# Expert weights five quarters ahead, raw words two parts ahead, a later exponential, and split words written in place

## The chip, the cores and the metric

The kernel runs on one core of a Trainium2 chip. The metric is the device time of one execution in microseconds (us), the median of several runs. Less is better.

## The reference

Three layers run one after the other. Only the second is touched by the change, and the third supplies the weights that one part of the change splits.

```python
# 1. gated recurrence over 768 steps, 4 batches x 8 heads of 40: x (3072 tokens, 320)
# 2. one of 8 experts per token (moe)
xn, en = x / (norm(x) + 1e-6), emb / (norm(emb) + 1e-6)
logits = xn @ en.T / tau
expert_idx = argmax(logits, axis=1)
gate_w = softmax(logits)[token, expert_idx]
for e in range(8):
    mask = expert_idx == e
    out[mask] = gate_w[mask, None] * (relu(x[mask] @ w1[e]) @ w2[e])   # 320 -> 1024 -> 320
# 3. rational layer (moe2): double words for w_in in memory
h = x @ w_in                                                          # 320 -> 2048
P = a0 + a1 h + a2 h^2 + a3 h^3;  Q = 1 + |b0||h| + |b1| h^2
out = (P / (Q + 1e-6)) @ w_out                                        # 2048 -> 320
```

The matrices w_in and w_out of layer 3 reach the core as 64-bit words, so each element is a low and a high 32-bit word side by side. Every product is made of three fast matmuls: each operand is split into a high part (rounded to the matmul's format) and a low part (the rest), and high by high, high by low and low by high are added in PSUM.

## The kernel before, in words

**Stages.** From 0 to about 216 us: the recurrence, the routing and the sorting of tokens by expert. From about 216 to 222 us: a branch on a register, around code for experts with more tokens than their buffer holds. That code is not run here, and each engine takes the branch by itself, once its own instructions before it are done. From there to about 458 us: the experts. Then to the end: the rational layer, with matmuls of 384 columns.

**The experts.** There are 64 blocks, n = 0 to 63. Block n is one eighth (`fb`) of the 1024 hidden units of expert `e`. The loop at the end of the listing issues per block, in this order: `gemm1(n)` (8 matmuls, L228, into `ph`), after which ScalarE (ACT) rounds the relu to `hh` (L1469) and VectorE (DVE) forms the rest `hl` (L1470); `gemm2(n-2)` (matmuls L1484 to L1486 into `yb`, with `hh` and `hl`); DMA loads; the transposes of the next expert's tokens (`x_prep`, PE L1107, ACT L1083 for the high part, DVE L1088 for the low part `xl`); the splitting of expert weights; and then a number of turns, each of which issues one step of the gates and one step of the split of layer 3's weights. Instructions keep this written order on every engine, and every engine runs its own list in order.

**Expert weights.** They come in quarters, two blocks each, 32 in all (`qq`). `w_load` issues four DMAs from SyncE (SP): `r1` (L162, L166 twice) and `r2` (L168), each with two buffers. `w_hi` makes the high parts `h1` and `h2` on ACT (L183, L185) three quarters ahead. `w_lo` makes the low parts `l1` and `l2` on GpSimd (POOL; L192, L196), partly on DVE at first. A buffer of `r1` or `r2` is free for a later load when both have read it. The load of quarter qq+4 is issued in the first block of quarter qq.

**Layer 3's weights.** `dbl` walks through 32 parts, 16 of w_in and 16 of w_out. `dbl_load` brings the raw words of a part into `raw` (L1357 and L1358, or L1361; two buffers; the load of part i+1 is issued after step 0 of part i). `dbl_split` has 8 steps: ACT L1386, DVE L1388, L1390, L1393, L1395, L1397 and L1406, and at last ACT L1409, or two stores from SP (L1412, L1413). L1393 reads the high words of `raw`, that is every second word, and L1395 its low words; L1395 writes `vt`, a buffer without gaps. `dbl_steps` spreads the steps over the blocks: most of them fall into blocks 8 to 40.

**The gates.** `gates` is a chain of short DVE steps on 128 rows, with one exponential on ACT (L1066) between L1064 and L1068. There is one such chain per expert, started in the last block of the expert before.

**Around it.** `x_load` gathers an expert's tokens (POOL), `y_scatter` scatters its results (POOL), and `y_load` (SP L1112) loads the sorted rows for layer 3 in block 52.

Of the kernel before, what the change touches and what calls it, by code (L numbers as in the profile page):

```python
# [8 lines left out]
F32 = mybir.dt.float32  # L9
F32R = mybir.dt.float32r  # L10
# [11 lines left out]
def kernel(  # L22
# [130 lines left out]
    def w_load(qq):  # L153
# [6 lines left out]
        cs = slice(qd * 256, (qd + 1) * 256)  # L160
        r1 = wsl.tile([128, 3, 256], F32, name="r1", tag="r1", bufs=2)
        nc.sync.dma_start(  # L162
            out=r1[:, 0:2, :], in_=w1r[bass.ds(e * DM, 256), cs].rearrange("(k p) f -> p k f", p=128)
        )
        for d in range(2):
            nc.sync.dma_start(out=r1[64 * d:64 * d + 64, 2, :], in_=w1r[bass.ds(e * DM + 256, 64), cs])  # L166
        r2 = wsl.tile([128, 2, DM], F32, name="r2", tag="r2", bufs=2)
        nc.sync.dma_start(  # L168
# [874 lines left out]

    def gates(pool, g, hd, tag, own=None):

# [18 lines left out]
        nc.vector.tensor_tensor(out=lg, in0=lg, in1=nrm.unsqueeze(2).broadcast_to([128, n, NE]), op=ALU.mult)  # L1064
        yield
        nc.scalar.activation(out=lg, in_=lg, func=AF.Exp)  # L1066
# [272 lines left out]
    with ExitStack() as mctx:  # L1339
        mp = mctx.enter_context(tc.tile_pool(name="mp", bufs=2, side="right"))  # L1340
        NB = NE * NFB
# [9 lines left out]
        def dbl_load(i):  # L1351
            raw = mp.tile([128, 3 * 128, 2], I32, name="raw", bufs=2)
            if i < 16:
# [12 lines left out]
        def dbl_steps(n):  # L1366

            a, c = (W0 * min(max(v - NFB, 0), 4 * NFB) + W1 * max(min(v, DE) - 5 * NFB, 0) for v in (n, NB))
            return a * ND * NS // c

        def dbl_split(i):
# [6 lines left out]

            if (i + 1) * NS <= dbl_steps(S3N[0]):
                st_ = vown[:, 0:n].bitcast(I32)  # L1380
            else:
                st_ = mp.tile([128, 384], I32, name="st_", bufs=1)[:, 0:n]
            vt = mp.tile([128, 384], F32, name="vt", bufs=1)[:, 0:n]
            ts, stt = nc.vector.tensor_scalar, nc.vector.scalar_tensor_tensor

            nc.scalar.activation(out=cf, in_=hi32.bitcast(F32), func=AF.Abs, scale=2.0**-112)  # L1386
            yield
            ts(out=st_, in0=c, scalar1=3, scalar2=-4096, op0=ALU.logical_shift_left, op1=ALU.bitwise_and)  # L1388
            yield
            stt(out=c, in0=hi32, scalar=-(2**31), in1=st_, op0=ALU.bitwise_and, op1=ALU.bitwise_or)  # L1390
            yield
# [24 lines left out]
        def dbl():  # L1416
            for i in range(ND):
                for k, _ in enumerate(dbl_split(i)):
                    if k == 0 and i + 1 < ND:
                        dbl_load(i + 1)  # L1420
                    yield
# [38 lines left out]
        def gemm1(n):  # L1460
# [5 lines left out]
            mm3(ph, h1, l1, slice(half * 128, half * 128 + 128), sx["x", e])  # L1466
            hh = mp.tile([128, 512], F32R, name="hh", bufs=4)[:, 0:c]
            hl = mp.tile([128, 512], F32R, name="hl", bufs=4)[:, 0:c]
            nc.scalar.activation(out=hh, in_=ph, func=AF.Relu)  # L1469
# [47 lines left out]
        x_load(1)  # L1517
        w_load(4)
        w_load(5)

# [32 lines left out]

        coef_load()
        dbl_load(0)
        dbls = dbl()

# [107 lines left out]
        for n in range(NB + LAG2):  # L1665
# [22 lines left out]
            if n >= NB:  # L1688
                continue
            if half == 0 and 5 < qq + 4 < 4 * NE:  # L1690
                w_load(qq + 4)
            if fb == 0 and 1 < e + 1 < NE:
# [20 lines left out]
            if n == 1 or fb == NFB - 1 and e + 1 < NE:  # L1713
                g = 0 if n == 1 else e + 1
                gs = slice(g * JS, g * JS + slots(g).stop)
                gsteps = gates(mp, gate[:, gs], head[:, gs, :], "g", vown[:, 384:] if g < NE - 1 else None)
            nd, ng = dbl_steps(n + 1) - dbl_steps(n), (4 if n > 5 else 6) if n else 0
            for i in range(max(nd, ng)):
# [132 lines left out]
```

## Time and profile before

| quantity | value |
|---|---|
| device time, median of 3 runs | 823.98 us (822.82 to 827.11) |
| the profiled execution's own device time | 823.25 us |
| its span in the profile | 821.2 us |
| mean granted clock of TensorE | 0.967 |
| busy: PE, DVE, POOL, ACT | 760.3, 713.6, 584.3, 488.8 us |

The span runs from the first to the last instruction that the profile shows; the device time is 2.05 us more. Times in the rows are microseconds from the start of the span. PE is the engine of the matmuls, and a stretch in which it is idle or at half its clock is where time can be had, as long as no other engine is then the next to be late.

### The profile page before, as it was taken

The page shows a single profiled execution, that of the slowest core. Times are in us where ns is not written, and L with a number is a line of the kernel's source. Part 1 is how long each engine was busy: PE and PEld are TensorE (multiplying, and loading weights), DVE is VectorE, ACT ScalarE, POOL GpSimd, SP SyncE. Part 2 cuts the span into 40 slices and gives each one's busy share as a digit, 9 for nine tenths or more (in the row PEclk, how much of TensorE's full clock was granted, in tenths as well). Part 3 has the DMA queues.
Part 4 walks back from the last instruction along what each step waited for, and adds up shares of the span by engine and source line. Part 5 has one row for each costly group of instructions (what it writes and reads, how often), then busy time and mean ns, then how long its engine had stood idle before and what let it go on. Part 6 is the DMA issues. An engine that isn't in the chain of part 4 may idle for free.

```text
span 821.2 us, 14468 instructions
## 1 busy us (share of the span) xinstructions
PE 760.3 (93%) x4724; PEld 707.2 (86%) x4724; DVE 713.6 (87%) x1421; ACT 488.8 (60%) x839; POOL 584.3 (71%) x595
## 2 busy tenths in 40 slices
PE   8889898978798999999989899999999999999994
PEld 5678776758687888989989799999999999999983
DVE  8999999998589999887777888989888888889882
ACT  5243433333364555455547887877787878777772
POOL 7664343563456767768962698989899898989883
PEclk9997999998799999999999899999999999999998
DMA  8998787742546757788766021101001010000000
GB/s 212 270 261 233 217 237 223 220 122 88 158 123 200 222 171 215 232 240 254 227 200 203 27 80 50 50 1 43 7 21 30 17 33 9 17 9 17 1 25 24
DMA packets 86964, 102.41 MB, mean 125 GB/s; under 512 B 7915, under 2 KB 79219, under 8 KB 86880
## 3 DMA queue, kind: packets, MB, share of 16 engines
q1 hardware_dynamic: 82976, 88.63, 37.4%
q0 software_dynamic: 3904, 12.77, 4.8%
q8 instruction: 39, 0.64, 0.4%
q14 instruction: 45, 0.37, 0.1%
HBM read 84.01 MB, written 17.93 MB: 124 GB/s over the span
## 4 chain that ended last, share of the span: by engine, by line
PE 49%; DVE 9%; issue 5%; POOL 4%; DMA 2%; ACT 2%; SPq 1%; POOLq 0%; DVEq 0%; ACTq 0%
PE h L228 21%; PE yb L1306 6%; PE yb L1304 6%; PE yb L1305 6%; PE ph L228 4%; DMA r<-in_w 2%; POOL l L192 1%; DVE hl L1470 1%; PE yb L1484 1%; PE yb L1486 1%; PE yb L1485 1%; PE h L1107 1%; DVE ct L1390 1%; DMA raw<-in_w_in 1%; DVE vown L1393 1%
## 5 line engine op out<-in xcount | busy, mean ns | idle before, releaser
L1244 POOL TENSOR_TENSOR U<-U,A 128x768 f32<-128x768 f32 (+1 forms) x65 | 119.3, 1836 | 29.8 <-ACT U L1236 25.2
L1306 PE MATMUL yb<-wo,gl 128*128 128x320 f32 x384 | 119.5, 311 | 1.8 <-POOL gl L1290 1.8
L1290 POOL TENSOR_TENSOR gl<-P,gh 128x768 fp32r<-128x768 f32 x63 | 118.1, 1875 | 3.6 <-ACT gh L1287 3.0
L1304 PE MATMUL yb<-wo,gh 128*128 128x320 f32 x384 | 119.1, 310 | 1.2 <-ACT gh L1287 1.2
L1305 PE MATMUL yb<-wo,gh 128*128 128x320 f32 x384 | 118.9, 310 | 0.0
L1220 ACT ACTIVATE P<-h,coef 128x768 f32<-128x768 f32 (+1 forms) x65 | 64.0, 985 | 72.2 <-PE h L228 72.2
L228 PE MATMUL h<-xh,winh 128*128 128x384 f32 x256 | 90.9, 355 | 3.9 <-DVE P L1253 3.8
L192 POOL TENSOR_TENSOR l<-r,h 128x384 fp32r<-128x384 f32 x64 | 63.7, 1017 | 43.2 <-ACT h L183 40.0
L228 PE MATMUL h<-xh,winl 128*128 128x384 f32 x256 | 86.7, 339 | 0.0
L228 PE MATMUL h<-xl,winh 128*128 128x384 f32 x256 | 86.7, 339 | 0.0
L1248 DVE TENSOR_TENSOR P<-P,h 128x768 f32<-128x768 f32 (+1 forms) x65 | 61.2, 942 | 27.9 <-ACT A L1228 23.2
L1306 PEld LDWEIGHTS yb<-wo,gl 128*128 128x128 f32 x384 | 72.5, 189 | 2.6 <-POOL gl L1290 2.6
L1304 PEld LDWEIGHTS yb<-wo,gh 128*128 128x128 f32 x384 | 72.6, 189 | 1.5 <-ACT gh L1287 1.5
L1305 PEld LDWEIGHTS yb<-wo,gh 128*128 128x128 f32 x384 | 72.5, 189 | 0.0
L1238 POOL TENSOR_SCALAR U<-A,coef 128x768 f32<-128x768 f32 x56 | 55.2, 985 | 21.3 <-ACT A L1228 20.7
L1484 PE MATMUL yb<-h,hh 128*128 128x320 f32 (+1 forms) x216 | 68.0, 315 | 2.5 <-DVE hl L1470 1.4
L1485 PE MATMUL yb<-l,hh 128*128 128x320 f32 (+1 forms) x216 | 67.2, 311 | 0.0
L1253 DVE SCALAR_TENSOR_TENSOR P<-P,coef,h 128x768 f32<-128x768 f32 (+1 forms) x65 | 65.2, 1003 | 2.3
L1486 PE MATMUL yb<-h,hl 128*128 128x320 f32 (+1 forms) x216 | 67.2, 311 | 0.0
L228 PE MATMUL ph<-xh,h 128*128 128x256 f32 (+4 forms) x152 | 55.4, 364 | 10.0 <-DVE hl L1470 5.1
L1279 DVE SCALAR_TENSOR_TENSOR P<-P,coef,s 128x768 f32<-128x768 f32 (+1 forms) x62 | 62.0, 1000 | 1.7
L1271 DVE SCALAR_TENSOR_TENSOR U<-U,s 128x768 f32<-128x768 f32 (+1 forms) x62 | 58.0, 935 | 4.8 <-ACT s L1267 4.6
(596 smaller groups left out, 2319.5 us busy)
## 6 DMA issues: line engine op xcount, KB each, us to landing
fb<-fz_d SPq DMA_DIRECT2D x22, 512.0 KB
r<-in_w SPq DMA_DIRECT2D x32, 320.0 KB
r<-in_w SPq DMA_DIRECT2D x32, 256.0 KB
raw<-in_w_out SPq DMA_DIRECT2D x16, 320.0 KB
r<-in_w SPq DMA_DIRECT2D x64, 64.0 KB
raw<-in_w_in SPq DMA_DIRECT2D x32, 128.0 KB
x_rows<-xt SPq DMA_DIRECT2D x24, 164.5 KB
xt<-y_sorted SPq DMA_DIRECT2D x8, 481.5 KB
```

Of the source, the lines that this page charges most:

```text
L192: eng.tensor_tensor(out=l1[:, :, sl], in0=r1[:, :, sl], in1=h1[:, :, sl].bitcast(F32), op=ALU.subtract)
L228: mms = [nc.tensor.matmul(ps, lhsT=a, rhs=b, start=(i == 0), stop=(i == 7)) for i, (a, b) in enumerate(seq)]
L1220: r = nc.scalar.activation(out=part("P", m, i), in_=part("ph", m, i), func=AF.Identity, scale=coef[:, 3:4], bias=coef[:, 2:3])
L1244: eng.tensor_tensor(out=U, in0=U, in1=part("A", m, i), op=ALU.mult)
L1253: r = nc.vector.scalar_tensor_tensor(out=P, in0=P, scalar=coef[:, 1:2], in1=part("ph", m, i), op0=ALU.add, op1=ALU.mult)
L1290: eng.tensor_tensor(out=part("gl", m, i), in0=part("P", m, i), in1=part("gh", m, i).bitcast(F32), op=ALU.subtract)
L1304: nc.tensor.matmul(y, lhsT=gh[:, i, t], rhs=wh, start=first, stop=False)
L1305: nc.tensor.matmul(y, lhsT=gh[:, i, t], rhs=wl, start=False, stop=False)
L1306: nc.tensor.matmul(y, lhsT=gl[:, i, t], rhs=wh, start=False, stop=last)
L1484: nc.tensor.matmul(y, lhsT=hh[:, js], rhs=h2[:, half, :], start=(fb == 0), stop=False)
L1485: nc.tensor.matmul(y, lhsT=hh[:, js], rhs=l2[:, half, :], start=False, stop=False)
L1486: nc.tensor.matmul(y, lhsT=hl[:, js], rhs=h2[:, half, :], start=False, stop=(fb == NFB - 1))
```

## The change

Five edits, all in the stage of the experts and just ahead of the branch:

1. `w_load` runs five quarters ahead instead of four. Every third quarter from the sixth on takes its `r1` and `r2` from another pool, so there are three buffers of each. The load of quarter 6 is issued ahead of the branch.
2. `raw` has three buffers, and `dbl_load` runs two parts ahead; two parts are loaded ahead of the branch.
3. The exponential of the gates comes four turns later (three for the first expert), and blocks 1 to 5 have seven gate turns instead of six.
4. The separate buffers `vt` and `st_` go. `vt` is written over the low words in `raw`, so L1395 now writes every second word and L1406 reads every second word; for the last two parts, `st_` is written over the high words.
5. `hh` and `hl` have three buffers instead of four.

```diff
         cs = slice(qd * 256, (qd + 1) * 256)
-        r1 = wsl.tile([128, 3, 256], F32, name="r1", tag="r1", bufs=2)
+        pool, bufs = (sx["mp"], 1) if qq > 5 and qq % 3 == 0 else (wsl, 2)
+        r1 = pool.tile([128, 3, 256], F32, name="r1", tag="r1", bufs=bufs)
         nc.sync.dma_start(
...
             nc.sync.dma_start(out=r1[64 * d:64 * d + 64, 2, :], in_=w1r[bass.ds(e * DM + 256, 64), cs])
-        r2 = wsl.tile([128, 2, DM], F32, name="r2", tag="r2", bufs=2)
+        r2 = pool.tile([128, 2, DM], F32, name="r2", tag="r2", bufs=bufs)
         nc.sync.dma_start(
...
-    def gates(pool, g, hd, tag, own=None):
+    def gates(pool, g, hd, tag, own=None, turns=0):
...
         nc.vector.tensor_tensor(out=lg, in0=lg, in1=nrm.unsqueeze(2).broadcast_to([128, n, NE]), op=ALU.mult)
-        yield
+        for _ in range(1 + turns):
+            yield
         nc.scalar.activation(out=lg, in_=lg, func=AF.Exp)
...
     with ExitStack() as mctx:
-        mp = mctx.enter_context(tc.tile_pool(name="mp", bufs=2, side="right"))
+        sx["mp"] = mp = mctx.enter_context(tc.tile_pool(name="mp", bufs=2, side="right"))
         NB = NE * NFB
...
         def dbl_load(i):
-            raw = mp.tile([128, 3 * 128, 2], I32, name="raw", bufs=2)
+            raw = mp.tile([128, 3 * 128, 2], I32, name="raw", bufs=3)
             if i < 16:
...
-            if (i + 1) * NS <= dbl_steps(S3N[0]):
-                st_ = vown[:, 0:n].bitcast(I32)
-            else:
-                st_ = mp.tile([128, 384], I32, name="st_", bufs=1)[:, 0:n]
-            vt = mp.tile([128, 384], F32, name="vt", bufs=1)[:, 0:n]
+            st_ = vown[:, 0:n].bitcast(I32) if (i + 1) * NS <= dbl_steps(S3N[0]) else hi32
+            vt = lo32.bitcast(F32)
             ts, stt = nc.vector.tensor_scalar, nc.vector.scalar_tensor_tensor
...
             yield
-            ts(out=st_, in0=c, scalar1=3, scalar2=-4096, op0=ALU.logical_shift_left, op1=ALU.bitwise_and)
+            s3 = c if st_ is hi32 else st_
+            ts(out=s3, in0=c, scalar1=3, scalar2=-4096, op0=ALU.logical_shift_left, op1=ALU.bitwise_and)
             yield
-            stt(out=c, in0=hi32, scalar=-(2**31), in1=st_, op0=ALU.bitwise_and, op1=ALU.bitwise_or)
+            stt(out=c, in0=hi32, scalar=-(2**31), in1=s3, op0=ALU.bitwise_and, op1=ALU.bitwise_or)
             yield
...
                 for k, _ in enumerate(dbl_split(i)):
-                    if k == 0 and i + 1 < ND:
-                        dbl_load(i + 1)
+                    if k == 0 and i + 2 < ND:
+                        dbl_load(i + 2)
                     yield
...
             mm3(ph, h1, l1, slice(half * 128, half * 128 + 128), sx["x", e])
-            hh = mp.tile([128, 512], F32R, name="hh", bufs=4)[:, 0:c]
-            hl = mp.tile([128, 512], F32R, name="hl", bufs=4)[:, 0:c]
+            hh = mp.tile([128, 512], F32R, name="hh", bufs=3)[:, 0:c]
+            hl = mp.tile([128, 512], F32R, name="hl", bufs=3)[:, 0:c]
             nc.scalar.activation(out=hh, in_=ph, func=AF.Relu)
...
         x_load(1)
-        w_load(4)
-        w_load(5)
+        for qq in (4, 5, 6):
+            w_load(qq)
...
         coef_load()
-        dbl_load(0)
+        for i in range(2):
+            dbl_load(i)
         dbls = dbl()
...
                 continue
-            if half == 0 and 5 < qq + 4 < 4 * NE:
-                w_load(qq + 4)
+            if half == 0 and 6 < qq + 5 < 4 * NE:
+                w_load(qq + 5)
             if fb == 0 and 1 < e + 1 < NE:
...
                 gs = slice(g * JS, g * JS + slots(g).stop)
-                gsteps = gates(mp, gate[:, gs], head[:, gs, :], "g", vown[:, 384:] if g < NE - 1 else None)
-            nd, ng = dbl_steps(n + 1) - dbl_steps(n), (4 if n > 5 else 6) if n else 0
+                gsteps = gates(mp, gate[:, gs], head[:, gs, :], "g", vown[:, 384:] if g < NE - 1 else None, 4 if g else 3)
+            nd, ng = dbl_steps(n + 1) - dbl_steps(n), (4 if n > 5 else 7) if n else 0
             for i in range(max(nd, ng)):
```

Lines after the edits stand up to four lines later in the listing of the changed kernel (L162 is L164 there, L168 is L170, L1066 is L1070, L1112 is L1116, L1361 is L1365, L1386 is L1387, L1412 is L1414, L1469 is L1471).

The lists of instructions of TensorE and GpSimd keep their order. Three places show what moves on the others.

SyncE ahead of the branch, before: the load of quarter 5, then the coefficients of layer 3, one part of raw words (four DMAs) and the register load for the branch.

```order
L162 DMA r_2600<-in_w 128x2x256
L166 ISA
L166 DMA r_2600<-in_w 64x256
L166 ISA
L166 DMA r_2600<-in_w 64x256
L168 ISA
L168 DMA r_2604<-in_w 128x2x320
L1137 DMA coef<-in_ra 128x4
L1138 DMA coef<-in_rb 128x2
L1357 DMA raw<-in_w_in 128x256
L1358 DMA raw<-in_w_in 64x256
L1357 DMA raw<-in_w_in 128x256
```

The same place after, from the last DMA of quarter 5 on:

```order
L170 DMA r_2604<-in_w 128x2x320
L164 ISA
L164 DMA r_2606<-in_w 128x2x256
L168 ISA
L168 DMA r_2606<-in_w 64x256
L168 ISA
L168 DMA r_2606<-in_w 64x256
L170 ISA
L170 DMA r_2610<-in_w 128x2x320
L1141 DMA coef<-in_ra 128x4
L1142 DMA coef<-in_rb 128x2
L1361 DMA raw<-in_w_in 128x256
```

Quarter 6 (r_2606, r_2610) has come in, and behind these rows stand eight raw DMAs instead of four: SyncE has eight DMAs more to issue before it reaches the branch.

SyncE late in the stage, before. In this piece r2_6722 belongs to quarter 29, raw_6770 is part 29 of the split, xt4 is the load of sorted rows, and r1_6798 belongs to quarter 30.

```order
L168 ISA
L168 DMA r2_6722<-in_w2 128x2x320
L1412 DMA wouth_d_2550<-ct_6646 128x320
L1413 DMA woutl_d_2551<-lo3_6736 128x320
L1361 DMA raw_6770<-in_w_out 128x640
L1112 DMA xt4_6796<-y_sorted_87 128x3x321
L162 ISA
L162 DMA r1_6798<-in_w1 128x2x256
```

The same place after; r2_6702 belongs to quarter 30, raw_6748 is part 30, and r1_6774 belongs to quarter 31.

```order
L170 ISA
L170 DMA r2_6702<-in_w2 128x2x320
L1414 DMA wouth_d_2550<-ct_6627 128x320
L1415 DMA woutl_d_2551<-lo3_6716 128x320
L1365 DMA raw_6748<-in_w_out 128x640
L1116 DMA xt4_6772<-y_sorted_87 128x3x321
L164 ISA
L164 DMA r1_6774<-in_w1 128x2x256
```

At the same stores and the same load of sorted rows stands the quarter that came two blocks later before, and the raw part that came one part later; quarter 30's `r1` and `r2` now stand ahead of the load of sorted rows.

ScalarE around the exponential of the second expert, before:

```order
L1386 ACTIVATE ct_4677<-raw_4624 128x384
L1469 ACTIVATE hh_4693<-ph1_119 128x512
L185 ACTIVATE h2_4662<-r2_4545 128x640
L1066 ACTIVATE head_84<-head_84 128x4x8
L1469 ACTIVATE hh_4730<-ph0_118 128x512
L1102 ACTIVATE xt4_4547<-xt4_4547 128x4x64
L1083 ACTIVATE xh0_4758<-pt_4752 128x512
L183 ACTIVATE h1_4762<-r1_4655 128x768
L1409 ACTIVATE winh_4251<-ct_4677 128x3x128
```

The same place after:

```order
L1387 ACTIVATE ct_4686<-raw_4581 128x384
L1471 ACTIVATE hh_4701<-ph1_119 128x512
L187 ACTIVATE h2_4671<-r2_4490 128x640
L1471 ACTIVATE hh_4735<-ph0_118 128x512
L1106 ACTIVATE xt4_4558<-xt4_4558 128x4x64
L1087 ACTIVATE xh0_4763<-pt_4757 128x512
L185 ACTIVATE h1_4767<-r1_4552 128x768
L1411 ACTIVATE winh_4262<-ct_4686 128x3x128
L1070 ACTIVATE head_84<-head_84 128x4x8
```

The exponential stands five rows later, behind the `hh` of the next block, the next expert's transposed tokens and a weight split. The exponential of the first expert keeps its place on ScalarE; the other seven move like this one.

## Rows read from the trace of the kernel before

**Rows 1.** The page's first part: engine, busy us, share of span, instructions.

```profile
PE 760.3 (93%) x4724; PEld 707.2 (86%) x4724; DVE 713.6 (87%) x1421; ACT 488.8 (60%) x839; POOL 584.3 (71%) x595
```

**Rows 2.** Busy time by stretch: engines with instruction counts, granted clock, DMA share, GB/s.

```profile
218.00:220.00 2.00, 0.00 (x0) 0.00 (x0) 0.00 (x0) 0.00 (x0) 1.06 (x2) 0.50 0.99 286
239.00:345.00 106.00, 100.28 (x562) 89.48 (x561) 98.38 (x228) 58.07 (x111) 75.15 (x86) 1.00 0.69 202
345.00:390.00 45.00, 43.95 (x270) 41.67 (x269) 36.11 (x97) 22.49 (x45) 33.94 (x39) 1.00 0.85 257
412.00:418.00 6.00, 3.19 (x20) 2.95 (x20) 2.08 (x6) 2.70 (x7) 2.94 (x5) 1.00 0.98 297
418.00:422.00 4.00, 3.95 (x17) 3.95 (x18) 4.00 (x12) 1.31 (x4) 3.92 (x6) 0.62 0.49 178
```

**Rows 3.** Waits of PE, 230 to 460 us: total us, times, longest.

```profile
PE ph L228 <- DVE hl L1470: 5.1, 4, 2.7
PE pt L1107 <- DVE xl L1088: 4.0, 4, 1.8
PE h L228 <- DVE P L1253: 3.8, 1, 3.8
```

**Rows 4.** Timeline of PE: start, duration, and in brackets idle before and releaser.

```profile
327.28 0.33 PE L1107 MATMUL pt<-ident,xt 128*128 128x128 f32 x1 [0.61 <-DVE xl L1088]
...
349.63 0.47 PE L228 MATMUL ph<-xh,h 128*128 128x448 f32 x1 [0.27 <-DVE hl L1470]
...
357.68 0.33 PE L1107 MATMUL pt<-ident,xt 128*128 128x128 f32 x1 [0.64 <-DVE xl L1088]
...
412.19 0.43 PE L228 MATMUL ph<-xh,h 128*128 128x352 f32 x1 [0.41 <-DVE hl L1470]
...
418.05 0.43 PE L228 MATMUL ph<-xh,h 128*128 128x352 f32 x1 [2.67 <-DVE hl L1470]
```

**Rows 5.** Timeline of DVE, three stretches.

```profile
316.82 0.56 DVE L1388 TENSOR_SCALAR vown<-ct 128x384 int32<-128x384 int32 x1 [0.48 <-issue]
...
348.52 0.49 DVE L1388 TENSOR_SCALAR vown<-ct 128x320 int32<-128x320 int32 x1 [1.87 <-issue]
...
416.55 0.49 DVE L1388 TENSOR_SCALAR vown<-ct 128x320 int32<-128x320 int32 x1 [3.85 <-ACT ct L1386]
```

**Rows 6.** Timeline of ACT, three stretches.

```profile
316.24 0.55 ACT L1386 ACTIVATE ct<-raw 128x384 f32<-128x384 f32 x1 [2.14 <-DMA raw<-in_w_in]
...
347.99 0.50 ACT L1386 ACTIVATE ct<-raw 128x320 f32<-128x320 f32 x1 [4.16 <-DMA raw<-in_w_out]
...
410.49 0.74 ACT L185 ACTIVATE h<-r 128x640 fp32r<-128x640 f32 x1 [3.77 <-DMA r<-in_w]
...
415.30 0.84 ACT L183 ACTIVATE h<-r 128x768 fp32r<-128x768 f32 x1 [3.36 <-DMA r<-in_w]
```

**Rows 7.** Timeline of SP's DMA queue: start and duration of an issue.

```profile
216.84 0.49 SPq L1358 DMA_DIRECT2D raw<-in_w_in  x1
228.94 0.41 SPq L162 DMA_DIRECT2D r<-in_w  x1
...
405.58 0.40 SPq L168 DMA_DIRECT2D r<-in_w  x1
...
409.82 0.39 SPq L162 DMA_DIRECT2D r<-in_w  x1
```

**Rows 8.** Timeline of POOL, around 404 us.

```profile
403.83 1.72 POOL L196 TENSOR_TENSOR l<-r,h 128x320 fp32r<-128x320 f32 x2
```

**Rows 9.** Waits of ACT, 230 to 460 us.

```profile
ACT head L1066 <- DVE head L1064: 13.9, 7, 3.9
```

**Rows 10.** Three lines' instructions: count, ns shortest/median/longest, first and last start, forms.

```profile
L1388 DVE TENSOR_SCALAR vown<-ct x30: 495/561/563, 244.1 to 416.5; 128x384 int32<-128x384 int32 x16, 128x320 int32<-128x320 int32 x14
...
L1393 DVE TENSOR_SCALAR vown<-raw x30: 486/560/564, 245.6 to 418.0; 128x384 int32<-128x384 int32 x16, 128x320 int32<-128x320 int32 x14
...
L1395 DVE SCALAR_TENSOR_TENSOR vt<-raw,vown x19: 473/553/555, 246.2 to 344.8; 128x384 f32<-128x384 uint32 x16, 128x320 f32<-128x320 uint32 x3
```


## The prediction

> **What bounds the kernel now.** I read the busy shares first: the reader is to see that PE works 93% of the span [rows 1], so the change can win only where PE stands still or runs at half its clock. The edits touch the stage of the experts, 222 to 458 us, so the second view is busy time by stretch [rows 2]. Three kinds of stretch stand there. From 239 to 345 us PE and DVE are both nearly full: DVE is busy 98.38 of 106 us, and the other 7.62 us over its 228 instructions are 0.033 us each, the gap from one instruction to the next. From 345 to 390 us DVE has slack (36.11 of 45) and the DMA share is 0.85. From 412 to 418 us PE works only 3.19 of 6 us while the DMA share is 0.98, and from 418 to 422 us the granted clock is 0.62.
>
> The third view is PE's waits in that stage [rows 3]. In all of them PE waits for DVE: for `hl` (the largest 2.7 us), for `xl`, and once, at the change to the rational layer, 3.8 us for P. The change makes no DVE instruction of those shorter; it can only let DVE start sooner. So for each stall the question is whether DVE was itself waiting, or simply had too much to do. The timeline of PE gives the stalls one by one [rows 4], and DVE's timeline answers: ahead of the stall at 327, of those at 349 and 358, and of the large one at 418 us, DVE sat idle for 0.48, 1.87 and 3.85 us in front of a split step, L1388 [rows 5]. Ahead of the others (the rest of the 5.1 and 4.0 us of rows 3) DVE had no idle time beyond its gaps, but for the first of the stage, which stands behind the first expert's exponential; that one keeps its place on ACT.
>
> The fourth view, ACT's timeline, says why DVE was idle [rows 6]. At 316.24 and 347.99 us ACT had waited 2.14 and 4.16 us for raw words, and L1388 reads what ACT makes of them. At 410.49 us it had waited 3.77 us for quarter 29's `r2`, and at 415.30 us 3.36 us for quarter 30's `r1`; `hh` stands behind both in ACT's list, and `hl` behind `hh`. So PE's stalls at 412.19 and 418.05 us end with two weight loads. Those were late because they were issued late: SP issued quarter 29's `r2` at 405.58 us and quarter 30's `r1` only at 409.82 us, behind two stores, a raw load and the load of sorted rows [rows 7], landing 4.9 and 5.5 us later. The first had waited for its buffer: its last reader is the low part of quarter 27, the POOL instructions that begin at 403.83 us and end at 405.55 us [rows 8].
>
> **The change part by part.** The sum is made against the profiled execution, 823.25 us (span 821.2 and 2.05 around it), which lies 0.73 us under the median of 823.98.
>
> Weights ahead. With a third buffer, quarter 29 no longer waits for the low part of quarter 27 but for that of 26, two blocks sooner; quarter 30 takes the place that quarter 29 had, so its last load goes out at about 405.6 us and lands near 410.5 us. It is wanted near 411 us, when ACT now reaches quarter 30 some 4 us earlier than at 415.30. Quarter 31's `r1` is then issued where quarter 30's was, near 409.8 us, and wanted two blocks later; that is what is late next, with a landing near 415 us against a need near 414, and there DVE has slack. I take both stalls as gone: 0.41 + 2.67 = 3.08 us. The cost on SP is nothing new: each load is moved, none added.
>
> Half clock. After the stall of 2.67 us the granted clock is 0.62 over the 4 us from 418 to 422 [rows 2], between its two levels of 1.2 and 2.4 GHz; PE was busy throughout. With the clock whole, the work of these 4 us takes 4 x 0.62 = 2.48 us. In every other stretch of rows 2 in which PE hardly stopped, the granted clock is 1.00. So if the stall goes, 1.52 us go with it.
>
> Raw words ahead. The waits at 316.24 and 347.99 us end when a part lands that was issued a part earlier; two parts ahead it has a whole part more (eight steps; a part takes 5.9 us on average, since 30 of them start from 244.1 to 416.5 us in rows 10). I take the DVE idle times as gone. The first was 0.48 us inside the saturated stretch, and PE's next stall, 0.61 us at 327.28, shrinks by 0.48. The second had cost the stalls of 0.27 and 0.64 us, together 0.91, for DVE has slack behind it. In the saturated stretch nothing else is to be had, because there the stalls come from DVE's work itself.
>
> Exponential. ACT waits 13.9 us in seven waits for L1064 ahead of it [rows 9], but DVE and PE lose nothing by these: where DVE is full, `hl` is late by DVE's own list, and no stall of rows 4 has this wait ahead of it. Four turns later ACT has done other work by then, and the DVE steps behind the exponential are the same in number. In the saturated stretch moving them shifts stalls and does not shorten the list. I take 0; bounds: 0.5 us better (the short steps L1068 and L1070 would no longer stand ahead of an `xl`) and 0.5 us worse. It is hidden by ACT's own idle time, 58.07 busy of 106 us [rows 2].
>
> Loads ahead of the branch. SP has eight more DMAs to issue there, each about half a microsecond (0.49 at 216.84 us), so it reaches the branch some 4.4 us later. It was last to be needed: its next DMA after the branch went out at 228.94 us, 12 us after the last one before [rows 7]. This cover hides the issues; if it were gone it would cost SP up to 4.4 us, but not PE, which does not wait for SP there. I take 0; the DMA traffic is the third rival.
>
> Written in place. L1395 writes every second word, and L1406 reads every second one. No row shows a strided write. For a strided read there is one: L1393 reads every second word of `raw`, L1388 reads words without gaps; their medians are 560 and 561 ns and their longest 564 and 563 [rows 10]. So the nearest row says 0, which I take for both lines. The other end: a write at half rate. By L1388's forms, 64 elements more cost 561 - 495 = 66 ns, 1.03 ns each, so it would add 0.40 us for 384 elements and 0.33 for 320. This is the second place where I chose, and it makes the fourth rival. For the last two parts three steps (L1388, L1393, L1397) write or read in place: under 1 us in all, behind 420 us where DVE has slack; 0.
>
> On this the Trainium skill speaks against the change: "Vector Engine (DVE) Microarchitecture Reference", section "5.2 Measured stream behaviour on trn2", says that a port keeps its full rate only in runs of two or more neighbouring 4-byte words, and gives, in place of 1.054 ns per column, 1.71 where the destination hops 4 KiB at every element and 2.50 where it steps by 24 words. By these, as estimates from the page, the 7104 elements of the 19 instructions from 239 to 345 us would cost 4.7 or 10.3 us, and the sum would be -1.3 or +4.3 us. But by the same rule L1393 would be slower than L1388, and rows 10 deny it for reads at this stride.
>
> Fewer `hh` and `hl`: `gemm1(n)`, after which a pair is written, stands behind `gemm2(n-3)`, its buffer's last reader, on PE's own list, so the wait is met when it is asked. 0.
>
> Sum: -3.08 - 1.52 - 0.91 - 0.48 = -5.99. On the profiled execution 823.25 - 5.99 = 817.3; from the median 823.98 - 5.99 = 818.0, which I predict. This case's own range is 816 to 819.9.
>
> **The rivals.**
>
> More is won (814 to 815). The stall of 3.8 us ahead of the rational layer [rows 3] is also shortened, because the last experts finish their loads and splits earlier. If it went by nearly all: 818.0 - 3.8 = 814.2. For it: that wait too is one for DVE. Against: it is for DVE's own chain to P, which no load of this change feeds.
>
> The transfers are the limit, not their issue (820 to 823.5). From 412 to 418 us the DMA share is 0.98 and from 345 to 390 us 0.85 [rows 2]; loads asked for sooner then only queue longer, the more so as the load of sorted rows and the scatters share the time. If the weights arrive as now, and only the raw words' 1.39 us are won, 823.98 - 1.39 = 822.6. Against: from 239 to 345 us the share is 0.69, so there is room for the queue to get ahead, and the bytes are the same.
>
> The start is delayed (820 to 822). From 218 to 220 us no engine but POOL does anything, the DMA share is 0.99 at 286 GB/s [rows 2], and PE comes out of the branch late. The change puts one quarter and one raw part more into this stretch: by the tile shapes 704 KB and 384 KB, 1.11 MB, 3.9 us at 286 GB/s. If PE's way past the branch waits for all of it: 818.0 + 3.9 = 821.9. Against: SP issues most of it only from 217 us on, when much of what the branch waits for is already on its way. The Trainium skill, "Runtime: NRT & Kernel Launch", section "Instruction fetch mechanics", says that a taken branch out of the fetched window forces a DMA fetch, which would make this wait one of DMA traffic; the rows show only that DMA is full there.
>
> The other side: the write over `raw` runs at half rate (824 to 826). The place is L1395 in the saturated stretch, 239 to 345 us, with 19 of its instructions: 16 x 0.40 + 3 x 0.33 = 7.4 us, all on the path since DVE is full there. 818.0 + 7.4 = 825.4. It decides from 5.99 / 7.4, so from about 0.33 us more per write on. For it: nothing shows such a write. Against: rows 10, for reads. If L1406's strided read cost as much again it would be 832.8, which those rows deny.
>
> **How the numbers follow.** Forecast 0.50, more is won 0.09, transfers 0.20, start 0.12, strided write 0.09. The bound of what a measurement of this kernel can tell from no change is about 0.5%, 4.1 us: faster lies below 819.9, slower above 828.1. Faster: nearly all of the forecast, all of the first rival, and 0.02 of the second and third: 0.60. Slower: what the strided write holds above its price, and something not thought of: 0.07. Same: 0.33. The range of 8 in 10 leaves out half of the first rival and the strided write: 814.2 to 824.4.
>
> **What would show it.** In the profile after: no idle time of PE over 0.5 us from 405 to 425 us, with granted clock 1.00 there; ACT's waits for `r` near nothing and its waits for raw words much shorter than now; L1395 with a median near 550 ns (near 950 if the fourth rival holds); PE's first block after the branch at the same time as now, 222 us, or up to 4 us later by the third; the stall ahead of the rational layer unchanged near 3.8 us. I am wrong if the loads of quarters 29 to 31 still land after ACT wants them, or if a new wait on PE stands between 239 and 345 us.

## The result and the profile after

The changed kernel took 818.2 us (median of 5 runs, 816.36 to 820.56), the kernel before 823.98 us (5 runs beside them): a ratio of 0.9917, 95% interval 0.989 to 0.9944. Run again on another occasion it took 818.91 us against 826.15, ratio 0.9905 (0.9882 to 0.9927). The forecast was 818.0 us.

First, PE where it had stood still before. The rows are PE's timeline of the changed kernel at the first matmul of blocks 55 to 58; a bracket would show idle time.

```profile
408.28 0.41 PE L230 MATMUL ph<-xh,h 128*128 128x352 f32 x1
...
410.97 0.32 PE L230 MATMUL ph<-xh,h 128*128 128x352 f32 x1
...
413.81 0.41 PE L230 MATMUL ph<-xh,h 128*128 128x352 f32 x1
...
416.74 0.41 PE L230 MATMUL ph<-xh,h 128*128 128x352 f32 x1
```

None has a bracket: the stalls of 0.41 and 2.67 us in [rows 4] are gone. The same stretches as in [rows 2], after (busy time, granted clock, DMA share, GB/s):

```profile
412.00:418.00 6.00, 6.00 (x43) 5.99 (x42) 5.93 (x14) 4.42 (x10) 4.51 (x7) 1.00 0.44 158
418.00:422.00 4.00, 3.97 (x27) 3.70 (x26) 3.94 (x13) 1.65 (x4) 3.38 (x4) 1.00 0.61 182
```

PE is busy throughout, the clock is whole, and the DMA share of 0.98 has become 0.44. SP's queue shows why; compare [rows 7]:

```profile
403.23 0.40 SPq L170 DMA_DIRECT2D r<-in_w  x1
...
405.52 0.37 SPq L1116 DMA_DIRECT2D xt<-y_sorted  x1
406.17 0.39 SPq L164 DMA_DIRECT2D r<-in_w  x1
```

The first row is quarter 30's `r2`, issued ahead of the load of sorted rows, and the last is quarter 31's `r1`. Before, quarter 30's `r1` was issued only at 409.82 us. ACT's timeline has no wait for a weight load any more (in [rows 6] it had 3.77 and 3.36 us), and none for raw words. Where it waits in the split it is now mostly for a store:

```profile
348.39 0.49 ACT L1387 ACTIVATE ct<-raw 128x320 f32<-128x320 f32 x1 [3.99 <-DMA wouth_d<-ct]
```

PE's waits from 230 to 460 us, to be held against [rows 3]:

```profile
PE h L230 <- DVE P L1257: 3.8, 1, 3.8
PE yb L1486 <- DVE ysb L1500: 2.9, 3, 1.6
PE ph L230 <- DVE hl L1472: 2.0, 2, 1.7
PE pt L1111 <- DVE xl L1092: 1.8, 2, 1.4
```

The wait for P is as long as before. What is left of the others lies almost all between 230 and 317 us, where DVE is full. The prediction named a new wait on PE between 239 and 345 us as a sign of being wrong. The line of `yb` has grown from 0.8 to 2.9 us, but its two large waits (1.58 us at 284.24, 1.13 at 316.17) stand in blocks 18 and 26, where PE waited before as well (1.44 us at 282.19, put down to `hl`, and 0.23 and 0.79 at 312.70 and 314.20). So they are not new.

The write in place, as [rows 10] showed it before:

```profile
L1397 DVE SCALAR_TENSOR_TENSOR raw<-raw,vown x30: 459/548/556, 248.3 to 414.1; 128x384 f32<-128x384 uint32 x16, 128x320 f32<-128x320 uint32 x14
```

Its median is 548 ns; written without gaps it was 547 over the same 30 instructions of before, 553 in the 19 of [rows 10]. And the branch, in PE's timeline of before and of after:

```profile
221.15 0.55 PE L228 MATMUL ph<-xh,h 128*128 128x256 f32 x1 [4.84 <-PEq L1560]
```

```profile
223.56 0.55 PE L230 MATMUL ph<-xh,h 128*128 128x256 f32 x1 [4.59 <-PEq L1563]
```

PE waits no longer at the branch than before, so the additional loads do not hold it up there. But it comes there 2.4 us later. This lag is older than the additional loads: a row of DVE ahead of them, before and after, and SP's first additional load, the `r1` of quarter 6, after.

```profile
211.59 0.22 DVE L219 TENSOR_REDUCE cnt<-ptmp 128x8 f32<-128x64 f32 x1
```

```profile
214.25 0.22 DVE L221 TENSOR_REDUCE cnt<-ptmp 128x8 f32<-128x64 f32 x1
```

```profile
217.11 0.37 SPq L164 DMA_DIRECT2D r<-in_w  x1
```

The execution was 2.66 us behind at 214.25 us, and that load was issued only at 217.11. And the start varies without the change: three of the kernels below (the exponential alone, in place alone, sorted rows later) run the same instructions up to the branch as the kernel before, and the first block starts in their profiles at 221.06, 223.48 and 226.38 us. Over all profiles it varies from 221.06 to 227.22. So most of what separates one execution from another arises ahead of the stage that was changed. From here on I read the stage by itself: the **stretch** from the first matmul of block 8 to that of block 63. Its ends in the profile of before:

```profile
239.17 0.40 PE L228 MATMUL ph<-xh,h 128*128 128x512 f32 x1
...
441.60 0.32 PE L228 MATMUL ph<-xh,h 128*128 128x352 f32 x1
```

and of after:

```profile
241.31 0.40 PE L230 MATMUL ph<-xh,h 128*128 128x512 f32 x1
...
436.08 0.32 PE L230 MATMUL ph<-xh,h 128*128 128x352 f32 x1
```

That is 202.43 us before and 194.77 after: 7.66 us shorter, more than the sum of 5.99. (A block's length is the time from its first matmul to that of the next block.)

### The profile page after: what moved, and what is told of

Same layout as the page of the kernel before. It is cut to its first block, busy times and chain, and to the rows that moved or that the text cites. A ratio compares the mean times of both kernels' runs of the same rounds, so it can differ in the third digit from the quotient of the medians.

```text
span 818.5 us, 14472 instructions
## 1 busy us (share of the span) xinstructions
PE 762.4 (93%) x4724; PEld 710.6 (87%) x4724; DVE 712.9 (87%) x1421; ACT 489.8 (60%) x839; POOL 579.3 (71%) x595
## 4 chain that ended last, share of the span: by engine, by line
PE 54%; DVE 7%; issue 4%; DMA 2%; POOL 2%; ACT 2%; SPq 1%; POOLq 0%; DVEq 0%; ACTq 0%
PE h L230 21%; PE ph L230 6%; PE yb L1308 6%; PE yb L1310 6%; PE yb L1309 6%; PE yb L1486 2%; PE yb L1488 2%; PE yb L1487 2%; DMA raw<-in_w_in 1%; DMA r<-in_w 1%; PE h L1111 1%; DVE hl L1472 1%; PE pt L1111 1%; DVE ct L1392 1%; DMA xt<-x_rows,xid 1%
## 5 line engine op out<-in xcount | busy, mean ns | idle before, releaser
L1308 PE MATMUL yb<-wo,gh 128*128 128x320 f32 x384 | 120.6, 314 | 1.2 <-ACT gh L1291 1.2
L1309 PE MATMUL yb<-wo,gh 128*128 128x320 f32 x384 | 120.3, 313 | 0.0
L1308 PEld LDWEIGHTS yb<-wo,gh 128*128 128x128 f32 x384 | 74.0, 193 | 1.5 <-ACT gh L1291 1.5
L1309 PEld LDWEIGHTS yb<-wo,gh 128*128 128x128 f32 x384 | 73.8, 192 | 0.0
```

Of the source, the lines that this page charges most:

```text
L1308: nc.tensor.matmul(y, lhsT=gh[:, i, t], rhs=wh, start=first, stop=False)
L1309: nc.tensor.matmul(y, lhsT=gh[:, i, t], rhs=wl, start=False, stop=False)
```

## The experiments

Ratios are to the kernel before, run on the same chip, with the 95% interval.

| kernel | stretch, us | against before | time, ratio (interval) |
|---|---|---|---|
| before | 202.43 | | 1 |
| changed | 194.77 | -7.66 | 0.9917 (0.989 to 0.9944) |
| changed, again | 194.53 | -7.90 | 0.9905 (0.9882 to 0.9927) |
| weights ahead alone | 199.35 | -3.08 | 0.994 (0.9921 to 0.9959) |
| raw words ahead and in place alone | 199.06 | -3.37 | 0.9952 (0.9926 to 0.9977) |
| raw words ahead, buffers apart | 199.09 | -3.34 | 0.9991 (0.9973 to 1.0009) |
| exponential alone | 201.17 | -1.26 | 1.0007 (0.999 to 1.0025) |
| in place alone | 206.21 | +3.78 | 1.0072 (1.0047 to 1.0098) |
| changed without weights ahead | 199.06 | -3.37 | 0.9984 (0.9963 to 1.0005) |
| changed without raw words ahead | 203.07 | +0.64 | 1.0024 (1.0007 to 1.0042) |
| changed without the exponential | 194.75 | -7.68 | 0.993 (0.9905 to 0.9955) |
| sorted rows loaded later | 201.58 | -0.85 | 1.0008 (0.9984 to 1.0031) |
| changed, split 5:3 | 192.97 | -9.46 | 0.9895 (0.9864 to 0.9925) |
| changed, split 3:2 | 193.89 | -8.54 | 0.9898 (0.9868 to 0.9928) |

The two profiles of the changed kernel differ by 0.24 us in the stretch. In time, the two kernels with raw words ahead have the same stretch within 0.03 us and ratios 0.4% apart: the order of small effects is therefore read from the stretch.

Of the kernel before there is only one profile, so whatever was peculiar to that execution stands in every difference against it. Block 55 shows it: it took 3.25 us there and 2.68 us in each of the thirteen other profiles, also where the weights come four quarters ahead. The stall of 0.41 us at its end (412.19 us in [rows 4]) is in none of them. So 0.57 us of every difference against before is not shown to come from an edit. Differences between two of the other kernels are free of this.

**The changed kernel again.** No edit.

> The changed kernel once more, for a second profile. In the first one the granted clock of the first 20 us was 0.70 (0.91 before), the first block after the branch began 2.4 us later than before, and the matmuls of the last 5 us ran at half clock; from that first block to block 58 it was 8.2 us shorter than before. If start and end are accidents of that execution: first block at 221 to 222 us, the stretch from it to block 58 again 8 us shorter than before, and a median about 6 to 8 us under that of before. If the change itself delays the start (the theory of loads ahead of the branch): first block again at 223 us or later, with the loss behind 205 us and not in the first 20.

First block at 224.49 us, from there to block 58 193.38 us. So the stage repeats, and the median was 7.2 us under that of before. The first block was late again, as the second expectation had it, but not for its reason: the same row of DVE stands at 215.31 us here, 3.72 us later than before, and SP issues the first additional load only at 218.22 us. The first block is 3.34 us late, so nothing was added behind that row.

**Weights ahead alone.**

```diff
-        r1 = wsl.tile([128, 3, 256], F32, name="r1", tag="r1", bufs=2)
+        pool, bufs = (sx["mp"], 1) if qq > 5 and qq % 3 == 0 else (wsl, 2)
+        r1 = pool.tile([128, 3, 256], F32, name="r1", tag="r1", bufs=bufs)
...
-                w_load(qq + 4)
+                w_load(qq + 5)
```

> The kernel before with the expert weights five quarters ahead and three buffers for hh and hl, nothing else. My theory: PE's stalls at 412 and 418 us and the half clock behind them go, 3.08 + 1.52 = 4.6 us; the stalls at 327, 349 and 358 us stay (0.61, 0.27, 0.64); 819.4 us from a median of 823.98. Rival of the transfers: the loads of quarters 29 and 30 land as late as before, ACT waits over 2 us for each, and the time is within 1 us of before.

Blocks 55 to 57 took 8.45 us instead of 13.61: the stalls and the half clock went, 5.16 us, of which 0.57 are those of block 55. ACT waits for no expert weight any more, so the rival of the transfers falls. But blocks 42 and 43 became 3.26 us longer, and ACT's timeline shows a late raw part there:

```profile
378.25 0.49 ACT L1387 ACTIVATE ct<-raw 128x320 f32<-128x320 f32 x1 [5.65 <-DMA raw<-in_w_out]
```

PE's timeline behind it:

```profile
379.58 0.42 PE L1485 MATMUL yb<-h,hh 128*128 128x320 f32 x1 [1.64 <-ACT ysb L1503]
```

ACT had waited for the same part before too (3.83 us, part 24), but could begin on it 0.24 us into block 42; here it is 1.97 us. SP issued the load of this part 0.53 us ahead of block 41 before and 0.78 us into block 41 here, behind the same sequence of DMAs. Why it was issued later this run does not show. I had not foreseen this new wait of PE.

**Raw words ahead, with the split in place.**

```diff
-            raw = mp.tile([128, 3 * 128, 2], I32, name="raw", bufs=2)
+            raw = mp.tile([128, 3 * 128, 2], I32, name="raw", bufs=3)
...
-                        dbl_load(i + 1)
+                        dbl_load(i + 2)
...
+            vt = lo32.bitcast(F32)
```

> The kernel before with three raw buffers, two parts ahead, and the words split in place, nothing else. My theory: ACT's waits for raw words shrink, the DVE idle times at 317 and 349 us go, PE's stalls at 327, 349 and 358 us shrink by 1.4 in all; 822.6 us. Rival of the exponential: those xl stalls (327, 358) hang on the gate steps that stand ahead of xl on DVE, so they stay, and at most 0.3 us is won. The stalls at 412 and 418 us stay by both.

3.37 us, more than twice what I had expected. All of ACT's waits for raw words are gone (31.4 us in 16 waits before). Block 29 is 0.36 us shorter and 34 to 38 together 1.05, which is what I had counted; and blocks 41 and 42 0.8, 55 and 56 0.9, which I had not. But blocks 35, 36, 50 and 55, 1.3 us of the 3.37, are just as short in the kernel with in place alone, where ACT waits longer for raw words than before; that part is not shown to be theirs. The rival, that the `xl` stalls hang on the exponential and stay, falls in this form, since they shrink without it. But they hang on it too: block 29 shrinks by 0.36 us here and by 0.84 in the next kernel, block 37 by 0.86 here and 0.51 there.

**The exponential alone.**

```diff
-        yield
+        for _ in range(1 + turns):
+            yield
         nc.scalar.activation(out=lg, in_=lg, func=AF.Exp)
```

> The kernel before with the exponential four turns later, nothing else. My theory: 0, within 0.5 us of before. Rival of the exponential: in the profile of the change the xl stalls at 263, 327 and 358 us shrank by 0.5, 0.6 and 0.6, because the short steps behind the exponential no longer stand ahead of xl on DVE; then this kernel alone wins 1.5 to 2.2 us, and blocks 13, 29 and 37 are shorter by 0.5, 0.8 and 0.9 us.

The stretch is 1.26 us shorter. Blocks 13, 29 and 37 are shorter by 0.5, 0.8 and 0.5, blocks 17, 18, 34, 42 and 50 longer by 1.6 in all, blocks 55 to 57 shorter by 1.0. The rival misses: the gains at blocks 13 and 29 are there, but other blocks pay for them. My theory, 0 within 0.5 us, is not settled by the stretch, since without the 0.57 us of block 55 there remain 0.69; the time shows no difference, as it would have it.

**The changed kernel without weights ahead.** `w_load(qq + 5)` is `w_load(qq + 4)` again, with two buffers and quarter 6 loaded in the loop.

> The changed kernel with the weights four quarters ahead again, all else as changed. Stage here means the time from the first block behind the branch to block 63: 220.45 us before, 212.5 changed. If the parts add up (weights alone -3.25, raw alone -3.39, exponential alone -1.39): stage 215.8. If raw words and weights share one SP queue, so that the weights' gain is only whole with raw words ahead (the weights alone made a new stall of 3.3 us at blocks 42 and 43, behind a raw part), then the weights are worth 5.2 here: stage 217.4 to 217.7, with the stall of 2.7 us ahead of block 57 and the half clock back.

The stretch is 4.29 us longer than in the changed kernel, and the first block to block 63 took 216.66 us, between the two expectations: the stall ahead of block 57 is back with 2.19 us and block 57 is at 4.49 us again.

**The changed kernel without raw words ahead.** `dbl_load(i + 1)` and two raw buffers again; the split stays in place.

> The changed kernel with two raw buffers, one part ahead, all else as changed. If the parts add up: stage 212.5 + 3.4 = 215.9. If the stall at blocks 42 and 43 is made by the weights running ahead of the raw words: it is back here with 2 to 3.3 us, ACT waits over 4 us for a raw part near 378 us, and the stage is 215 to 216.5. If it was an accident of the weights' run: stage at most 214.

The stretch is 8.30 us longer than in the changed kernel and longer than before; the first block to block 63 took 219.89 us, over both expectations. ACT waited 5.92 us for a raw part near 381 us, as the theory of the weights' run had it, but also in 25 places in all, 59.1 us together. So more than the weights' run was at work, and the next kernels looked for it.

**The changed kernel without the exponential.** `turns` is out again.

> The changed kernel with the exponential in its old place, all else as changed. My theory (0): stage 212.5 as with it. Rival, by the exponential alone: blocks 5 and 13 longer by 0.4 and 0.5, blocks 17 and 18 shorter by 0.45 in all, blocks 29 and 37 unchanged if the raw words have taken their stalls already: stage 212.9 to 213.9.

The stretch is the same to 0.02 us. The exponential's place still moves time between blocks: in its old place blocks 13 and 29 are 0.49 and 0.46 us longer, and blocks 17, 18 and 34 together 0.9 shorter. In the sum nothing is left.

**Sorted rows loaded later.** The kernel before with one step moved:

```diff
-            if n == NB - 12:
-                y_load(0)
...
                 w_load(qq + 4)
+            if n == NB - 12:
+                y_load(0)
```

> The kernel before with one step moved: the load of sorted rows, in block 52, is issued behind the load of quarter 30 and not ahead of it. If quarter 30 was late because it was issued late: it is issued 1.9 us sooner, lands near 413.4 instead of 415.3, and the stall ahead of block 57 shrinks from 2.7 to about 0.8 us, perhaps with a whole clock behind it: stage 217 to 218.6. If the DMA engines were the limit (share 0.98 from 412 to 418 us): quarter 30 lands less than 0.7 us sooner and the stage stays above 219.7.

SP issued quarter 30's `r1` at 413.24 us, and ACT could use it at 418.89:

```profile
413.24 0.39 SPq L162 DMA_DIRECT2D r<-in_w  x1
```

```profile
418.89 0.85 ACT L183 ACTIVATE h<-r 128x768 fp32r<-128x768 f32 x1 [2.79 <-DMA r<-in_w]
```

Block 55 begins at 414.81 us here and at 408.94 before. Against that, the issue is 2.45 us sooner (-1.57 for 0.88) and the landing 2.28 us sooner (4.08 for 6.36). The landing follows the issue: from issue to use it is 5.65 us here and 5.48 before. So quarter 30 was late because it was issued late, though what part of those 5.5 us is a queue in the DMA engines is not shown. The stage took 219.66 us, longer than the 217 to 218.6 of the first expectation and just under the bound of the other (219.7). Blocks 56 and 57 are 2.66 us shorter together; but block 58 is 1.80 us longer, and PE waits for the sorted rows themselves:

```profile
421.68 0.52 PE L1107 MATMUL pt<-ident,xt 128*128 128x128 f32 x3 [1.43 <-DMA xt<-y_sorted]
...
428.08 0.42 PE L1484 MATMUL yb<-h,hh 128*128 128x320 f32 x1 [1.38 <-ACT ysb L1502]
```

Of what another order in the same queue wins for one load, the next one here loses a large part.

**In place alone.** The kernel before with `vt` and `st_` over `raw`, which keeps two buffers.

```diff
-            vt = mp.tile([128, 384], F32, name="vt", bufs=1)[:, 0:n]
+            vt = lo32.bitcast(F32)
```

> The kernel before with the words split in place and three buffers for hh and hl, raw words still in two buffers and one part ahead. Stretch means the time from block 8 to block 63: 202.43 us before, 194.77 changed, 203.07 in the changed kernel without the raw words ahead. My theory on that last number: in place, a raw buffer is read until L1406 and not until L1395, two steps longer, so with two buffers the next load is issued two steps later and ACT waits more for raw words: here the stretch is 204 to 207 us, L1395 still takes 0.55 us at its median. Rival: that loss came from the weights running ahead alone, and in place costs nothing even with two buffers: 201.5 to 203.

3.78 us longer, inside what my theory gave (204 to 207 us), and slower in time: the interval of its ratio lies above 1. The instruction itself costs nothing here either (L1393 is L1395 of before):

```profile
L1393 DVE SCALAR_TENSOR_TENSOR raw<-raw,vown x30: 474/548/559, 248.6 to 425.1; 128x384 f32<-128x384 uint32 x16, 128x320 f32<-128x320 uint32 x14
```

The loss is in ACT's waits for raw words. Here:

```profile
ACT ct L1383 <- DMA raw<-in_w_in: 30.9, 15, 5.3
ACT ct L1383 <- DMA raw<-in_w_out: 15.9, 8, 3.3
```

and before:

```profile
ACT ct L1386 <- DMA raw<-in_w_out: 20.1, 9, 4.2
ACT ct L1386 <- DMA raw<-in_w_in: 11.3, 7, 4.7
```

46.8 us instead of 31.4. SP's queue names the reader that the next load waits for, from 239 to 400 us, before and here (L1404 here is L1406 of before):

```profile
SPq L1357 <- DVE vt L1395: 10.9, 7, 2.8
```

```profile
SPq L1357 <- DVE winl L1404: 13.9, 6, 5.4
```

A buffer that is also the scratch space is read two steps longer, until L1406, and its next load is issued after that.

**Raw words ahead, buffers apart.** Three raw buffers and two parts ahead, `vt` and `st_` as before.

> The kernel before with three raw buffers, two parts ahead, and three buffers for hh and hl, but with vt and st_ in buffers of their own as before. It tells what writing in place costs once there are three raw buffers. With in place (raw words ahead, split in place) the stretch from block 8 to block 63 was 199.06 us; in place with two buffers had cost 3.8 us. If three buffers hide the two steps longer that a buffer is held: 198.8 to 199.3 here, no more ACT waits for raw words than there. If part of that cost is still in the changed kernel: 197.5 or less here, and a kernel with vt apart would beat it.

199.09 us against 199.06 with the split in place (which had four pairs of `hh` and `hl`, this one three): in the stretch the third buffer hides the whole cost. In time neither is shown to beat the other; their intervals touch.

**Another spread of the split.** The changed kernel with

```diff
-        W0, W1 = 2, 1
+        W0, W1 = 5, 3
```

> The changed kernel with the steps of layer 3's split spread 5:3 over blocks 8 to 40 and the later ones, in place of 2:1 (about 181 of 256 steps in the first 32 blocks and not 190). If what is left of PE's stalls there (1.7, 0.5, 1.6 and 1.1 us in the profile of the change) is DVE's own work, each of 9 steps of 0.55 us moved out shortens it: stretch 191 to 193.5 us, down from 194.7. If DVE then becomes late in the later blocks, where it has 39 of 45 us busy: stretch 194.5 or more.

and with `W0, W1 = 3, 2`:

> The same with 3:2 (about 175 steps in the first 32 blocks). By the theory of DVE's own work: stretch 190 to 192.5 us, time 2 to 4 us under the changed kernel. By the rival (DVE late in the later blocks): the early stretch shrinks, but blocks 40 to 58 grow by as much, and the stretch is 194 or more.

The stretches are 1.80 and 0.88 us shorter than the first profile of the changed kernel. Blocks 8 to 39 take 120.77 and 121.28 us instead of 123.97, and blocks 40 to 58 take 56.08 and 56.50 instead of 54.68: the early blocks win and the later ones lose, so both theories hold for their part. 5:3 came out as the first of its expectations had it (191 to 193.5 us). 3:2 missed both of its own: it wins less than the first (190 to 192.5) and more than the second (194 or more), and its time is not shown to be under that of the changed kernel. What is left of PE's waits in the first of the two:

```profile
PE h L230 <- DVE P L1257: 3.8, 1, 3.8
PE pt L1111 <- DVE xl L1092: 2.1, 2, 1.4
PE ph L230 <- DVE hl L1472: 2.0, 2, 1.7
PE yb L1486 <- DVE ysb L1500: 1.1, 2, 0.6
```

The 5:3 kernel took 817.05 us against 824.68. It is the fastest kernel here by its stretch; in time its interval overlaps that of the changed kernel, so that it beats it is shown in the stage alone.

## Why the prediction was right, and where it was not

The time came out 0.2 us from the forecast, but that is closer than the argument deserves, and partly luck: the two occasions gave 5.8 and 7.2 us between the medians, and the stretch shrank by 7.7 to 7.9 us (7.1 to 7.3 without block 55), where the sum said 5.99.

- **Weights ahead.** Right, and the largest term: 4.60 forecast, 5.16 by the lengths of blocks 55 to 57 (13.61 to 8.45 us), 4.29 when undone, of which 4.00 lie in blocks 56 and 57. The stall of 0.41 us, put down to quarter 29's `r2`, is absent in every other profile, so it is not shown to be won by this. The half clock is part of it: block 57 went from 4.50 to 2.93 us, 1.57 for a forecast of 1.52. Missed: alone, 3.26 us of it went into a new wait at blocks 42 and 43, which is gone once the raw words come ahead too.
- **Raw words ahead.** Right in mechanism; the term was mis-sized: 1.39 forecast, 3.37 alone; without the 1.3 us that in place alone shows as well, about 2.0. In time the three kernels with raw words ahead and weights as before gave ratios of 0.9952, 0.9991 and 0.9984, only the first clear of 1. Part of the surplus was in the stalls that the timeline leaves unmarked. In PE's timeline of before, at the end of block 41:

```profile
371.32 0.31 PE L1486 MATMUL yb<-h,hl 128*64 128x320 f32 x1
371.77 0.44 PE L228 MATMUL ph<-xh,h 128*128 128x384 f32 x1
```

Such matmuls otherwise follow each other at 0.15 us, with rows of 0.31 us that overlap. Here it is 0.45, so 0.30 us were lost, and no bracket stands there. A bracket counts only from the modelled end of the matmul ahead. The same holds for the marked stalls: block 56 lost 3.02 us, of which the bracket showed 2.67.

- **Exponential.** 0 forecast; 0.02 in the change, 1.26 by itself, of which 0.57 are not shown to be its own. The account holds: the steps are moved and not saved, and blocks that win (13, 29) are paid for by others (17, 18, 34).
- **Written in place.** Right for the instruction: 548 ns, no half rate, so the fourth rival falls. Wrong in what I called its whole cost: the buffer is held two steps longer, which costs 3.78 us with two raw buffers and nothing with three. That is why undoing the raw words in the changed kernel costs 8.30 us: their own 3.37, these 3.78, and 1.15 that no run here separates.
- **Loads ahead of the branch.** Right: PE waited 4.59 us there, 4.84 before, and the late start in both profiles of the changed kernel was there before SP issued the first additional load; the third rival falls. The size of the cover was off: eight issues at 0.49 us are 3.9 us and not 4.4, and SP's last issue ahead of the branch came at 227.39 us, 10.55 later than before, of which only 2.4 are the late start. But its first load behind the branch went out at 231.86 us, 2.92 later than before, so next to nothing of it was left to be seen.
- **The transfers as the limit.** Falls: with weights ahead alone ACT waits for none of them, and where one load was issued 2.45 us sooner it landed 2.28 us sooner.
- **More is won at the rational layer.** Falls: 3.8 us before and after.
- **Fewer `hh` and `hl`.** Right as far as shown: no wait for a free pair appears, and the kernel with raw words ahead has the same stretch with three pairs as with four.

## What to carry to other kernels

Read a stall from the spacing of starts, block against block, and not from the idle time alone; and compare executions over the stage that was changed when what lies ahead of it varies by more than the effect. Where several streams share one issuing queue, look at all of them when one gets a further buffer: that one alone, or another order, can move the wait to the next stream, as it did with 3.26 of 5.16 us for the weights. A buffer that is reused as scratch space is paid for by the load that waits for it, so count how many steps longer it is held.

## What the runs showed of the hardware that was not expected

The start varied most: the granted clock of the first 20 us was 0.91 in the profile of before and 0.70 in that of the changed kernel, and the kernel with the sorted rows later, whose code up to the branch is that of before, had 0.70 as well and its first block 5.2 us later. The clock of these 20 us is not the whole of it, since 0.74 there went with a first block at 221.56 us in the kernel with raw words ahead. What decides it was not tried.

```profile
0.00:20.00 20.00, 17.81 (x85) 11.26 (x86) 17.03 (x37) 11.19 (x25) 15.37 (x59) 0.91 0.84 211
```

```profile
0.00:20.00 20.00, 17.34 (x57) 11.31 (x58) 14.25 (x28) 11.06 (x25) 13.38 (x55) 0.70 0.85 209
```

The first row is before, the second the kernel with the sorted rows later (busy time by stretch, with the granted clock behind the last bracket). Besides, a write to every second 4-byte word ran as fast as one without gaps (548 against 547 ns). The Trainium skill, "Vector Engine (DVE) Microarchitecture Reference", section "5.2 Measured stream behaviour on trn2", would have had it slower; at this step of two words the measurement decides against it.
